# Linear attention and a Sinkhorn-routed expert layer: attention products in 64x64 quarters, another feature order of x^T, and a new written order of the front

## The chip, the cores and the metric

The kernel runs on one core of one Trainium2 chip. The metric is device time in microseconds of one execution; the median of several executions is compared. The profile is of one further execution. Engines are named as in the profile: PE is TensorE's matmul, PEld its weight load, DVE VectorE, ACT ScalarE, POOL GpSimd, SP SyncE. A matmul takes a stationary operand (up to 128 partitions by 128 columns, loaded by PEld) and a moving operand of up to 512 columns. PE can also be addressed in quarters of 64 rows by 64 columns.

## The reference

```python
def _attn_ref(q, k, v):                        # 8 batches, 8 heads, 576 tokens, 64 features
    q_p, k_p = phi(q), phi(k)                  # phi(x) = (x if x > 0 else exp(x) - 1) + 1
    kv  = np.einsum('bhsd,bhse->bhde', k_p, v)
    z   = np.sum(k_p, axis=2)
    num = np.einsum('bhsd,bhde->bhse', q_p, kv)
    den = np.einsum('bhsd,bhd->bhs', q_p, z)[..., None] + 1e-06
    return num / den
def _moe_ref(x, w_gate, w1, w2):               # 4608 tokens, 512 features, 8 experts, 1024 hidden
    P = np.exp(x @ w_gate - max)
    for _ in range(8):
        P /= P.sum(1, keepdims=True) + 1e-09
        P /= P.sum(0, keepdims=True) + 1e-09
        P *= N / E
    for e in range(E):
        out += P[:, e:e + 1] * (np.maximum(x @ w1[e], 0.0) @ w2[e])
    return out
```

The attention output, with the 8 heads side by side, is x.

## The kernel before

**Attention.** `att(b, g)` (L366) treats four heads of one batch; there are 16 such calls. Partition p of an input tile holds nine consecutive tokens; partitions 0 to 63 belong to one head and 64 to 127 to the next (index hh), and a second index r selects the heads 4 further on. ACT takes Exp of k and q (L398, L463), DVE forms max(x + 1, 1) and the minimum with the Exp (L402, L406, L466, L470), which is phi. `f_kv` (L422) sums k' times [v, ones] over nine token slices with matmuls of 64x64 stationary size, four per slice in the four quarters of PE; two banks of PSUM and both partition halves receive them. `f_z` copies the result to `kvz`, in two copies of 64 partitions each (L440 to L444, the second after the first), into the diagonal blocks of a tile whose other blocks GpSimd zeroes once (L619). `f_qt` (L451) transposes q' in quarters, and `f_qc` (L472) copies it to SBUF. `heads` (L484) then multiplies: for each hh one full-array matmul of 288 token columns, with the two heads r = 0, 1 on the diagonal blocks of the stationary operand. It is called four times an `att`: two halves of the tokens (c), once for the denominator (`den`, written to the tile `att`) and once for the numerator (`num`). ACT takes Ln of the denominator (L499) and Exp of its negative (L504); DVE multiplies the numerator with it into x^T (L514). The resulting x^T has the feature index (64 r + d) on partitions and 2 g + hh as its chunk, so w1 and w_gate are loaded in matching pieces of 64 partitions (`load_w1` L327, `f_wg` L599). Tokens stand in the order 64 j + w for the token 9 w + j.

**Experts.** The 4608 tokens are nine groups of 512. A unit is one expert on one group: layer 1 (x^T to hidden) and layer 2. Expert 0 runs in the front while attention is still going on: `layer1` (L679) is plain in groups 0 to 4 and `block7` (L877) uses seven products (Winograd's form) in place of eight in groups 5 to 8. `unit_plain` (L987) has the plain layer 2 of eight products, each of four 512-column matmuls (L998); `unit` (L1059) calls `layer2` (L1067) with seven products of eight 256-column matmuls (L1114), four DVE sums S of the hidden activations (L1085), a seed copy on ACT (L1166) and evictions, four of them copies and two adds (L1132). The constant NS = 4 makes units 4 to 7 of expert 0 use it. `combos` makes the weight sums W and T. After that, experts 1 to 7 run with seven products in both layers (`pair`, L806; `layer2`). `last` (L1191) is the last layer 2, plain, in tiles whose finishing DVE pass is L1219, and `out_dma` (L969) stores each tile in two halves of 64 token rows.

**What sets the order.** Nothing is scheduled at run time. `_Plan` (L17) collects tasks with an engine, an estimated duration, dependences and buffers, and issues them engine by engine. PE's `TURN` is what the plan assumes for a change between tasks with `cfg=0` and `cfg=1` (quarters). The first 1811 tasks follow `_FRONT` (L141), a list written out by hand: task number and engine letter (p PE, a ACT, d DVE, g POOL, s SP, m a landing, n none). What follows is chosen by the plan's estimates. So the list fixes the order on every engine, the loads on POOL's queue among them, up to expert 2. The waits themselves are semaphores, and the estimates have no part in them.

Quarters in PE's list today: 20 islands of kv and transposes among full-array work, 16 of them behind the first layer-1 matmul. On POOL's queue eight loads of q, k, v stand ahead of the first piece of the first w1, and two loads on SP's.

Of the kernel before, what the change touches and what calls it, by code (L numbers as in the profile page):

```python
# [11 lines left out]
FP16 = mybir.dt.float16  # L12
# [5 lines left out]
class _Plan:  # L18
# [4 lines left out]
    TURN = 0.13  # L23
# [118 lines left out]
50s 51m 108n 61n 1n 113n 2p 48s 49m 3p 4p 5p 6p 7p 8p 9p 10p 11p 12p 13p 14p 15p 16p 17p  # L142
18p 62a 63d 54a 0g 19p 20p 21p 22p 23p 24p 25p 26p 27p 64d 55d 28p 65p 78g 79m 89n 52g 53m 56d
90a 57n 58p 59d 60d 76g 77m 66a 29p 82a 30p 31p 120g 121m 131n 67p 68a 32p 33p 34p 35p 36p 37p 69p
38p 39p 40p 83d 91d 84d 132a 133d 92d 80g 81m 85n 86p 134d 87d 88d 70a 71a 118g 119m 41p 93p 94a 42p
43p 74p 125d 75d 124a 95p 72p 44p 122g 123m 146g 147m 45p 96a 73d 126d 127n 153d 46p 97p 98a 99a 128p 129d
130a 135p 136d 109g 110m 148g 149m 159n 100p 596p 137p 101d 150g 151m 152a 154d 138a 160a 47p 102p 103d 155n 161d 162d
597p 598p 139p 140a 141a 111g 112m 156p 157d 158a 174g 175m 163p 164d 176g 177m 187n 595n 599p 144p 145d 165p 166a 600p
602p 601d 604p 603d 606p 167p 142p 180a 605d 168a 178g 179m 114g 115m 608p 610p 609a 612p 181d 143d 182d 189d 188a 190d
202g 203m 204g 205m 215n 613d 183n 184p 185d 611a 191p 192d 169a 186a 607a 614p 632n 615a 172p 173d 206g 207m 193p 194a  # L150
208a 618p 170p 171d 209d 210d 217d 234g 235m 245n 211n 195p 616p 216a 218d 633p 635p 636d 634a 196a 212p 197a 213a 219p
220d 214d 637p 639p 246a 638a 116g 117m 232g 233m 236g 237m 247d 260g 261m 262g 263m 200p 221p 222a 248d 201d 239d 640d
619p 626a 617p 238a 240d 223p 641p 198p 224a 225a 624a 199d 292g 293m 104g 105m 241n 643p 644a 266a 267d 249p 642d 273n
242p 243d 244d 275d 250d 645p 646a 620p 622p 647p 290g 291m 318g 319m 106g 107m 264g 265m 251p 623p 303n 304a 294g 295m
274a 252a 305d 268d 226p 276d 227d 253p 621p 228p 269n 254a 255a 648d 229d 230p 270p 320g 321m 348g 349m 296a 231a 271a
297d 628d 325d 306d 666p 277p 278d 376g 377m 272a 258p 259d 668p 653p 279p 324a 331n 665n 298d 630d 346g 347m 332a 256p
257d 299n 667a 280a 654p 281p 322g 323m 282a 669d 333d 352a 283a 300p 307p 301d 670p 302d 671a 672p 308d 309p 310a 284p
326d 285d 334d 651p 311p 673a 312a 286p 359n 360a 287d 652p 353d 313a 335p 336d 374g 375m 327n 328p 329a 330a 288p 289a
661a 387n 389d 404g 405m 350g 351m 378g 379m 406g 407m 460g 461m 674p 469s 337p 338a 354d 361d 362d 462g 463m 470s 314p
315d 649p 339p 675a 388a 340a 659a 316p 355n 560d 381d 317d 650p 676p 356p 390d 357d 341a 363p 408g 409m 364d 655p 358a  # L160
342p 417n 411d 419d 343d 493g 494m 380a 678p 365p 656p 344p 677d 410a 464g 465m 432g 433m 491g 492m 471s 500s 501s 366a
561d 382d 383n 562d 345d 553d 367p 680p 698n 681d 663a 679a 368a 418a 699p 700d 391p 384p 392a 385a 420d 386d 701p 703p
369a 393p 394a 554d 702d 412d 495g 496m 502s 684p 372p 373d 439d 555d 434g 435m 438a 657a 395p 705p 396a 445n 370p 371d
685p 563s 564m 421p 440d 704d 413n 476n 414p 682p 692a 706a 397a 688p 415a 416d 422a 400p 447d 478d 401d 707p 498d 423p
446a 424a 708a 556s 557m 567d 568d 569d 436g 437m 503g 398p 399d 683p 709p 570s 571m 425p 689p 711p 448d 477a 497a 690d
426a 710a 427a 574d 575d 441n 442p 443a 479d 576d 449p 450d 686p 713p 444d 451p 499d 565s 566m 572s 573m 577s 578m 558s
559m 579s 580m 508n 509a 510d 712a 687p 428p 452a 714a 696a 581d 582d 429d 583d 740p 742p 584s 585m 588g 589n 739n 590g
591m 743d 453p 741a 454a 455a 430p 431d 511d 504n 744p 480p 481d 746p 456p 457d 402p 403a 505p 694a 466a 745d 467d 506d
507d 468d 735d 748p 747a 749a 512p 458p 459d 750p 752p 751d 513a 472n 514p 515a 473p 474a 736d 516p 475d 517a 518a 753a
754p 755d 721p 519p 737d 520d 482p 483a 722p 729a 521p 522d 738d 756d 757d 484p 485a 486a 719p 489p 490d 717p 720p 727a  # L170
718p 725a 487p 488d 551n 592n 593g 594m 1009s 1010m 1011s 1012m 1013s 1014m 1015s 1016m 758d 778d 586s 587m 1017s 1018m 731d 715p
716p 723a 785n 779d 762p 763a 760p 523p 552p 761a 524a 732d 836d 780d 786p 781s 782m 783s 784m 787a 525n 1019s 1020m 766p
790p 791a 800p 801a 733d 837d 734d 792p 788p 793a 802p 803a 806p 796p 526d 759d 1001d 789a 797d 838d 839s 840m 808p 804p
807a 767a 805a 794p 809d 795d 764p 798p 799a 810p 527p 1002d 811d 528d 770p 771d 844p 845a 846p 812p 847a 813a 768p 850p
851a 765a 772p 843n 854p 773a 529d 858p 848p 894d 1003d 1021s 1022m 1051s 1052m 1053s 1054m 860p 818p 852p 849a 855d 814d 769d
859a 864p 862p 819a 820p 865a 863a 861a 815d 1004d 824p 868p 825a 856p 816d 857a 821a 853d 866p 817d 895d 869d 530p 896d
828p 902p 903a 826p 870p 871a 867d 531d 908p 909a 829d 822p 830p 831a 906p 532d 823a 952d 533p 872d 827d 904p 912p 905a
901n 907a 876p 953d 878p 916p 917a 913d 914p 534d 873d 918p 922p 954d 877a 897s 898m 955s 956m 923a 910p 882p 535d 874d
899s 900m 841s 842m 926p 911d 915a 920p 919a 924p 879a 883a 921a 925d 875d 960p 536p 537d 927d 886p 887d 961a 966p 1055s
1056m 957s 958m 967a 880p 964p 884p 928p 929a 970p 962p 963a 888p 889a 974p 968p 959n 965a 538d 539p 885d 930d 936p 975a  # L180
971d 972p 973a 540d 969d 541d 980p 976p 977a 934p 881a 981a 935a 982p 1023p 978p 984p 542p 979a 931d 940p 1024a 983d 985d
543d 1025p 986p 1029p 941a 937a 1026a 932d 944p 1030a 1031p 1027p 1028a 1033p 987a 544d 938p 545p 1034d 1035p 1037p 1036a 1038a 1032d
945d 1039p 1040a 546d 547d 933d 946p 1043p 1044a 1045p 1041p 1047p 1065p 548p 549d 550d 1046d 947a 988p 942p 1000n 1057s 1058m 943d
1059s 1060m 1048d 1042a 1061s 1062m 1063s 1064m 1066a 989p 996a 1147s 1148m 1149s 1150m 1067p 1068a 990p 1049p 1071p 1050a 1072a 1151s 1152m
1513n 1514g 1515m 728d 1005d 1006d 629a 1121d 991p 997a 992p 892a 1073p 994p 1122d 1007d 1069p 1123d 1074d 1070a 625a 1075p 627d 697a
993p 1076d 1077p 691d 1079p 1081p 664a 1080a 631d 1008d 1082a 1078a 995p 1085p 1086a 1087p 1083p 1089p 1093p 1095p 1124d 999d 1090d 1088d
998d 1091p 1084a 1094a 1099p 1096a 939d 1101p 1097p 1125p 1127p 1128d 695d 1092a 1100a 1129d 1126a 1130p 1131a 1103p 1135p 1138p 1104d 1105p
1107p 1136d 1098a 775d 1139d 1137d 662a 1109p 1141p 1106a 1108a 1113p 1153s 1154m 1155s 1156m 1110a 1115p 1114a 1133a 730a 1132g 1134g 1157s
1158m 1111p 1102d 1117p 1161p 1163p 1112a 1142d 1140d 1116d 1143d 1144p 1118d 1119p 1159s 1160m 1269s 1270m 1271s 1272m 1273s 1274m 1516n 1517g
1518m 1162a 1167p 1164a 658a 1120a 1169p 1168a 1165p 1146d 1145d 1189d 1190d 1193p 1195p 1194a 1198p 1171p 1203p 1166a 660a 1191d 1192d 1197d  # L190
726d 1196d 1201a 1202g 1199a 1206p 1172d 1173p 1174a 1175p 1176a 1177p 1178a 1205d 1204d 1209p 1181p 1182a 1183p 1179p 724d 1185p 1207d 1170d
1211d 1208d 1210d 1186d 1215p 693a 1217p 1212p 1187p 1243d 1200g 1244d 1214d 777d 1213d 1245d 774d 1246d 1180a 1216a 1221p 832a 1218a 1223p
1219p 1247p 1249p 1222a 1250d 1224d 1251d 1220a 1248a 1252p 1255a 1256g 951a 1188a 1225p 1226d 1184d 1257p 1259d 1260p 1258d 1519d 893d 1261d
1227p 1228a 1229p 1230a 1231p 1232a 833a 1263p 1235p 1237p 1275s 1276m 1233p 1236a 1239p 1253a 1264d 1520d 1521d 1265d 1277s 1278m 1279s 1280m
1281s 1282m 1283p 1391s 1392m 1393s 1394m 1285p 1266p 1240d 1234a 1284a 1238d 1241p 1289p 1286a 1291p 1287p 1395s 1396m 1242a 835a 1268d 1262d
1267d 1315p 1290a 1316a 1311d 1317p 1320p 1312d 1313d 1321a 1319d 1318d 1314d 1293p 1325p 1328p 776d 1294d 1295p 1288a 1327d 1330d 1326d 1329d
# [25 lines left out]
def kernel(  # L222
# [139 lines left out]

    def att_bank():
        return at2[:, (len(p_att["order"]) - 1) % 2]

    def att(b, g):  # L366
        n = 2 * b + g
        pr = n - 100.0
# [961 lines left out]
```

## Time and profile before

| | us |
|---|---|
| median of 3 runs (lowest, highest) | 954.69 (954.31, 955.13) |
| the profiled execution | 955.01 |
| its span | 953.2 |
| start of the first layer-1 matmul on PE | 22.14 |
| start of the first block product of unit 5 | 124.02 |
| start of the first product of expert 1's third step | 191.27 |
| start of the last products of `last` | 947.16 |

Shares of the span: PE 99%, DVE 81%, ACT 61%, POOL 15%. The granted clock of PE is 1.0. By stages the shares differ: from 40 to 100 us DVE and ACT are busy about 94% of the time, after 200 us about 80% and 57%. How to read it: the three starts cut the span into a start-up, the attention stage, a stage in which expert 0's later units run beside the Sinkhorn iterations, and experts 1 to 7. Busy time of PE includes overlap of pipelined matmuls, so distances between starts are used for prices.

### The profile page before, as it was taken

The numbers are of one execution on the slowest core, as the hardware profiler recorded it, in microseconds if no ns is written. First come the engines' busy times: TensorE is split into PE (matmuls) and PEld (weight loads), VectorE is DVE, ScalarE is ACT, GpSimd is POOL, SyncE is SP. The second block draws the span as 40 slices with busy tenths as digits, with TensorE's granted clock in tenths as the row PEclk, the third lists the DMA queues.
The fourth block names the chain that finished last, engine by engine and source line by source line (L and its number), as shares of the span: only waits on it lengthen the run. The fifth ranks groups of instructions, "written<-read, shape, count | busy, mean of one in ns | idle before, by whom it ended". The sixth has DMA issues, their size and how long they took to land.

```text
span 953.2 us, 19767 instructions
## 1 busy us (share of the span) xinstructions
PE 939.4 (99%) x7728; PEld 645.9 (68%) x7728; DVE 775.3 (81%) x1500; ACT 582.3 (61%) x1033; POOL 144.6 (15%) x209
## 2 busy tenths in 40 slices
PE   7999999999999999999999999999999999999997
PEld 3555588666677666766677666766667666776665
DVE  7899899979887888778888888878887888877775
ACT  7999766766655555555555555555555555555552
POOL 6442000011111111111111111111112111111110
PEclk9999999999999999999999999999999999999999
DMA  9999863452244222652226222652226422215544
GB/s 245 256 252 198 192 164 106 122 122 79 78 115 91 78 78 78 161 122 79 78 78 128 79 78 79 150 108 64 76 67 147 112 78 79 73 45 166 166 133 133
DMA packets 81513, 112.73 MB, mean 118 GB/s; under 512 B 7436, under 2 KB 45196, under 8 KB 81420
## 3 DMA queue, kind: packets, MB, share of 16 engines
q1 hardware_dynamic: 56844, 75.65, 26.0%
q0 software_dynamic: 23856, 34.78, 19.5%
q8 instruction: 60, 0.98, 0.4%
q10 hardware_dynamic: 720, 1.05, 0.3%
q14 instruction: 33, 0.27, 0.1%
HBM read 119.69 MB, written 17.69 MB: 144 GB/s over the span
## 4 chain that ended last, share of the span: by engine, by line
PE 92%; ACT 3%; DVE 2%; DMA 1%; POOL 1%; issue 1%; DVEq 0%; ACTq 0%; POOLq 0%
PE ye L1114 36%; PE hq L818 24%; PE R L818 12%; PE Zye L1114 6%; PE Zye L818 6%; PE ye L998 2%; PE hq L703 2%; DMA w<-in_moe_w_dram 1%; ACT rden L499 1%; ACT eq L463 1%; PE num_ps L486 1%; PE att L486 0%; PE hq L1210 0%; DVE xT L514 0%; PE att L531 0%
## 5 line engine op out<-in xcount | busy, mean ns | idle before, releaser
L1145 DVE SCALAR_TENSOR_TENSOR acc<-ye,P_sb,acc 128x256 f32<-128x256 f32 x620 | 268.3, 480 | 126.9 <-PE ye L1114 125.0
L1114 PEld LDWEIGHTS <-S 128*128 128x128 f16 x1984 | 194.0, 98 | 46.6 <-DVE S L1085 0.2
L1114 PE MATMUL ye<-T,S 128*128 128x256 f16 x1488 | 192.8, 273 | 0.0
L1155 POOL TENSOR_TENSOR acc<-acc,st 128x256 f32<-128x256 f32 x124 | 88.2, 731 | 633.8 <-ACT st L1152 622.6
L1114 PEld LDWEIGHTS <-hb 128*128 128x128 f16 x1584 | 155.0, 98 | 43.0 <-issue 1.3
L818 PEld LDWEIGHTS <-W 128*128 128x128 f16 x1248 | 122.1, 98 | 86.0
L849 ACT ACTIVATE hb<-hq 128x512 f16<-128x512 f32 x134 | 80.0, 597 | 141.0 <-PE hq L818 135.7
L818 PE MATMUL R<-xs,W 128*128 128x512 f16 (+1 forms) x560 | 150.1, 358 | 0.0
L818 PE MATMUL hq<-xs,W 128*128 128x512 f16 (+1 forms) x560 | 150.1, 358 | 0.0
L818 PE MATMUL hq<-xs,w 128*128 128x512 f16 (+1 forms) x560 | 139.8, 358 | 0.0
L818 PEld LDWEIGHTS <-w 128*128 128x128 f16 x936 | 91.6, 98 | 59.3 <-issue 0.5
L846 ACT ACTIVATE hb<-Zye 128x512 f16<-128x512 f32 x134 | 80.1, 598 | 40.4 <-PE Zye L818 40.3
L1152 ACT ACTIVATE st<-Zye,P_sb 128x256 f32<-128x256 f32 x124 | 52.4, 470 | 76.7 <-PE Zye L1114 76.5
L852 DVE CUSTOM_DVE_ANT_0 hb<-hq,sx 128x512 f16<-128x512 f32 x126 | 86.6, 687 | 15.5 <-PE hq L818 15.3
L839 ACT COPY sx<-hq 128x512 f32<-128x512 f32 x126 | 73.5, 584 | 35.3 <-PE hq L818 35.3
L835 ACT COPY Zye<-hq 128x512 f32<-128x512 f32 x134 | 77.8, 580 | 21.1 <-PE hq L818 20.7
L852 DVE CUSTOM_DVE_ANT_0 hb<-R,sx 128x512 f16<-128x512 f32 x126 | 86.5, 686 | 4.8 <-ACT sx L839 3.8
L1085 DVE TENSOR_TENSOR S<-hb 128x1024 f16<-128x1024 f16 x124 | 85.0, 685 | 5.1 <-ACT hb L849 5.0
L818 PE MATMUL Zye<-xs,w 128*128 128x512 f16 (+1 forms) x280 | 75.0, 358 | 0.0
L843 ACT COPY sx<-R 128x512 f32<-128x512 f32 x126 | 74.4, 591 | 0.0
L1114 PE MATMUL ye<-w,hb 128*128 128x256 f16 x528 | 68.4, 273 | 0.6 <-DVE acc L1145 0.5
L1114 PE MATMUL Zye<-w,hb 128*128 128x256 f16 x528 | 68.4, 273 | 0.0
(120 smaller groups left out, 966.2 us busy)
## 6 DMA issues: line engine op xcount, KB each, us to landing
xs<-xd SPq DMA_DIRECT2D x196, 256.0 KB, 3.5
kin<-in_k_dram POOLq DMA_DIRECT2D x15, 576.0 KB, 7.3
w<-in_moe_w_dram POOLq DMA_DIRECT2D x16, 512.0 KB, 7.7
out_dram<-acc SPq DMA_DIRECT2D x63, 128.0 KB, 2.4
w<-in_moe_w_dram POOLq DMA_DIRECT2D x7, 1024.0 KB, 10.2
xs<-xd SPq DMA_DIRECT2D x49, 128.0 KB, 3.3
vv<-in_v_dram POOLq DMA_DIRECT2D x16, 288.0 KB, 7.2
hb<-in_q_dram POOLq DMA_DIRECT2D x15, 288.0 KB, 7.7
```

The lines of the kernel that those rows point to most:

```text
L818: nc.tensor.matmul(dst_[:, p, :] if parts == 2 else dst_.rearrange("p a b -> p (a b)"), lhsT=lhs(p, c), rhs=blk[i](c), start=(first and p ...
L835: nc.scalar.copy(out=Zt[1], in_=gX["tile"])
L839: nc.scalar.copy(out=gs2["tile"], in_=gX["tile"])
L843: nc.scalar.copy(out=gs5["tile"], in_=gR["tile"])
L846: nc.scalar.activation(out=dst(0, 0), in_=Zt[1], func=AF.Relu)
L849: nc.scalar.activation(out=dst(1, 0), in_=gX["tile"], func=AF.Relu)
L852: nc.vector._custom_dve(TENSOR_ADD_SAT, out=out_, in0=ps, in1=sb, s0=3.0e38, s1=0.0)
L1085: nc.vector.tensor_tensor(out=Sx[:, i], in0=a0, in1=a1, op=op)
L1114: nc.tensor.matmul(bank(g_)[:, s, :], lhsT=lhs(s, kk), rhs=rhs(kk), start=(new and s == 0 and kk == 0), stop=(kk == 3), skip_group_check=True)
L1145: nc.vector.scalar_tensor_tensor(out=dst(), in0=bank(g_)[:, s, :], scalar=P_sb[:, gg, e:e + 1], in1=dst(), op0=ALU.mult, op1=ALU.add)
L1152: nc.scalar.mul(out=gst["tile"], in_=bank(g_)[:, s, :], mul=P_sb[:, gg, e:e + 1])
L1155: nc.gpsimd.tensor_tensor(out=dst(), in0=dst(), in1=gst["tile"], op=ALU.add)
```

## The change

All in one file; the written list is replaced as a whole. In words:

- `heads` issues four 64x64 matmuls of 288 columns (hh by r) in place of two full-array ones, with `cfg=1`. Its output has hh on partition halves and r on banks. `kvz` has no zero blocks: one copy for `f_z`, and the two memsets on POOL go.
- x^T has features in their natural order (chunk g + 2 r, partition 64 hh + d). w_gate is one load of 128 partitions, the first expert's w1 two loads of 512 columns each (every feature), the later experts' w1 two loads of two chunks each. `layer1` sums chunks in the order 0, 2, 1, 3.
- In the last batch (b = 7) the copy `f_qc` brings tokens to their natural order, so group 8 is stored with one DMA a tile, on SP's and ACT's queues in turn.
- NS = 6: units 4 and 5 of expert 0 have the plain layer 2. The four W and four T sums are made ahead of unit 5.
- `last` ends with a 256-column and two 128-column tiles in place of two 256-column ones.
- The plan's estimates change, and `_FRONT` has 2192 entries. PE's list now has 51 islands of quarters (mostly two tasks, such as a num beside a den); 87 changes of mode lie behind the first layer-1 matmul, where there were 32. Seven loads stand ahead of the first w1 piece on POOL's queue. The copy `f_qc` of the last batch is on ACT, twice.

The core of the diff:

```diff
-    NS = 4
+    NR = B - 1
+    NS = 6
...
-    kvz_t = [fp.tile([P, 2, 2, P], FP16, ...
+    kvz_t = [fp.tile([P, 2, 2, D], FP16, ...
...
+            return load_w(moe_w1, "w1", p_w1, [[((slice(None), slice(None), slice(512 * i, 512 * i + 512)),
+                                                 512 * i, [[F, P], [P * F, NDT], [1, 512]])] for i in range(2)], e, ...
+        return load_w(moe_w1, "w1", p_w1, [[((slice(None), slice(2 * i, 2 * i + 2)), 2 * i * P * F, [[F, P], [P * F, 2], [1, F]])]
+                                           for i in range(2)], e, ...
...
-        for r in range(2):
-            def f_z(e, r=r):
-                s = slice(64 * r, 64 * r + 64)
-                src = gkv["tile"][s, :, 0:2 * D].rearrange("p h (z d) -> p h z d", z=2)
-                dst = gz["tile"][s, :, :, 64 * r:64 * r + 64]
-                copy(e, dst, src if r == 0 else src[:, :, ::-1])
+        def f_z(e):
+            copy(e, gz["tile"], gkv["tile"][:, :, 0:2 * D].rearrange("p h (z d) -> p h z d", z=2))
...
+            if b >= NR:
+                copy(e, gq["tile"].rearrange("p h (w j) -> p h w j", j=NJ), qps().rearrange("p h j w -> p h w j"))
...
         def heads(dst, c, z):
             for hh in range(2):
-                nc.tensor.matmul(dst[:, hh, 0:CH], lhsT=gz["tile"][:, hh, z, :],
-                                 rhs=gq["tile"][:, hh, :, :].rearrange("p j w -> p (j w)")[:, CH * c:CH * c + CH],
-                                 start=True, stop=True)
+                for r in range(2):
+                    nc.tensor.matmul(dst[half(hh), r, 0:CH], lhsT=gz["tile"][half(r), hh, r ^ z, :],
+                                     rhs=gq["tile"][half(r), hh, CH * c:CH * c + CH], start=True, stop=True)
...
-                nc.vector.tensor_tensor(out=xT[:, 2 * g:2 * g + 2, S * b + CH * c:S * b + CH * c + CH],
+                nc.vector.tensor_tensor(out=xT[:, g:NDT:2, S * b + CH * c:S * b + CH * c + CH],
...
-    for t in kvz_t:
-        nc.gpsimd.memset(t, 0.0)
...
-            t1 = add(("pe", 0.2175 * (c1 - c0)), f_hq, deps=[tw1[0 if c1 == 2 else 1], ...
+            t1 = add(("pe", 0.2175 * (c1 - c0)), f_hq, deps=[tw1[0 if g == 0 and f < 4 else 1], ...
...
-        for i, (tt, c0, cw) in enumerate(((3, 0, 512), (2, 0, 512), (1, 0, 512), (0, 0, 256), (0, 256, 256))):
+        for i, (tt, c0, cw) in enumerate(((3, 0, 512), (2, 0, 512), (1, 0, 512), (0, 0, 256), (0, 256, 128), (0, 384, 128))):
```

More of the change, by code (lines that the diff above doesn't have):

```diff
@@ L290 @@
     vv_t = [fp.tile([P, 3, NJ, D], FP16, tag=f"vv{i}", name=f"vv{i}", bufs=1) for i in range(NV)]
-    kvz_t = [fp.tile([P, 2, 2, P], FP16, tag=f"kvz{i}", name=f"kvz{i}", bufs=1) for i in range(2)]
+    kvz_t = [fp.tile([P, 2, 2, D], FP16, tag=f"kvz{i}", name=f"kvz{i}", bufs=1) for i in range(2)]
     kvps = front.enter_context(tc.tile_pool(name="kvps", bufs=1, space=PSUM))
@@ L364, in att_bank, with half @@
         return at2[:, (len(p_att["order"]) - 1) % 2]
+    def half(i):
+        return slice(64 * i, 64 * i + 64)
     def att(b, g):
@@ L472, in f_qc @@
         def f_qc(e):
[L473 to L474 removed]
+            gq["tile"] = fp.tile([P, 2, S], FP16, tag="qpT", name="qpT")
+            if b >= NR:
+                copy(e, gq["tile"].rearrange("p h (w j) -> p h w j", j=NJ), qps().rearrange("p h j w -> p h w j"))
+            else:
+                copy(e, gq["tile"], at2.bitcast(FP16)[:, :, 0:S])
         gtq = S_.grp(p_tq)
@@ L617 @@
         nc.vector.memset(t[:, 1], 1.0)
-    for t in kvz_t:
-        nc.gpsimd.memset(t, 0.0)
     att(0, 0)
     att(0, 1)
-    for r in range(2):
-        gsw = S_.grp(p_sw)
-        ti = add(("pool", 0.8), lambda _, r=r: f_wg(_, r), acq=[gsw], use=[gsw], prio=-96.5, after=1.75)
-        wg_done.append(add(("dma", 0.3), lambda _: None, deps=[ti], use=[gsw], prio=-96.5, lat=2.15))
+    gsw = S_.grp(p_sw)
+    ti = add(("pool", 0.8), f_wg, acq=[gsw], use=[gsw], prio=-96.5, after=1.75)
+    wg_done.append(add(("dma", 0.3), lambda _: None, deps=[ti], use=[gsw], prio=-96.5, lat=2.15))
     w_t = {0: load_w1(0, prio=-290.0, parts=2)}
@@ L701, in f_hq @@
                     ghq["tile"] = hqp.tile([P, 512], FP32, tag="hq", name="hq")
-                for c in range(c0, c1):
+                for i in range(c0, c1):
+                    c = (0, 2, 1, 3)[i]
                     nc.tensor.matmul(ghq["tile"], lhsT=gw1["tile"][:, c, ts(f, P)], rhs=xT[:, c, ds(512 * g, 512)],
-                                     start=(c == 0), stop=(c == NDT - 1))
+                                     start=(i == 0), stop=(i == NDT - 1))
             def f_rl(eng, f=f, ghq=ghq):
@@ L969, in out_dma, with f_o @@
     def out_dma(g, tt, deps, c0=0, cw=DM):
-        for half in range(2):
-            def f_o(_, half=half):
-                bb, j = divmod(2 * (4 * g + tt) + half, NJ)
-                dst = AP(tensor=out.tensor, offset=(S * bb + j) * DM + c0, ap=[[NJ * DM, PW], [1, cw]])
-                eng = nc.scalar if g >= NG - 2 and half == 1 else nc.sync
-                eng.dma_start(out=dst, in_=acc[g][64 * half:64 * half + 64, tt, c0:c0 + cw])
+        r0 = P * (4 * g + tt)
+        whole = r0 >= NR * S
+        n_out[0] += 1
+        for half in range(1 if whole else 2):
+            def f_o(_, half=half, eng=nc.scalar if (n_out[0] % 2 if whole else g == NG - 2 and half) else nc.sync):
+                bb, j = divmod(2 * (4 * g + tt) + half, NJ)
+                if bb >= NR:
+                    dst = AP(tensor=out.tensor, offset=(r0 + 64 * half) * DM + c0, ap=[[DM, P if whole else PW], [1, cw]])
+                else:
+                    dst = AP(tensor=out.tensor, offset=(S * bb + j) * DM + c0, ap=[[NJ * DM, PW], [1, cw]])
+                eng.dma_start(out=dst, in_=acc[g][64 * half:64 * half + (P if whole else 64), tt, c0:c0 + cw])
             add(("sp", 0.45), f_o, deps=deps, prio=900.0)
@@ L1002, in unit_plain @@
                              prio=g + 0.1 * (2 * tt + half) + 0.65)
-                if g == NG - 1:
-                    h_users[0].append(ty[tt])
-                    h_users[1].append(ty[tt])
+                if g >= NG - 2:
+                    for i in range(2):
+                        h_users[2 * (NG - 1 - g) + i].append(ty[tt])
         for tt in range(4):
@@ L1042, in combos @@
                      prio=-900.0 if e > 1 else 4.5)
-        for i in range(4):
+        for i in range(4 if e > 0 or NS < NG - 1 else 0):
             def f_T(_, i=i):
```

232 lines of the change are left out of this document (120 added, 112 removed).

## The prediction

> **What bounds the kernel now.** I read the page first, then busy time by stage, then TensorE's timeline, then the waits and the end. The stages are cut at three starts on TensorE: its first useful layer-1 matmul (22.14 us), the first block product of unit 5 (124.02) and the first product of expert 1's third step (191.27), from where both orders issue the same sequence.
>
> ```profile
> span 953.2 us, 19767 instructions
> ...
> PE 939.4 (99%) x7728; PEld 645.9 (68%) x7728; DVE 775.3 (81%) x1500; ACT 582.3 (61%) x1033; POOL 144.6 (15%) x209
> ```
>
> ```profile
> 22.14:124.02 101.88, 98.60 (x1502) 55.68 (x1503) 92.80 (x162) 88.44 (x123) 28.80 (x43) 1.00 1.02 225
> 124.02:191.27 67.25, 67.25 (x564) 54.62 (x563) 63.41 (x137) 45.36 (x85) 1.26 (x2) 1.00 0.45 121
> 191.27:947.16 755.89, 755.32 (x5383) 526.41 (x5382) 602.88 (x1173) 432.29 (x811) 100.03 (x140) 1.00 0.37 99
> ```
>
> Columns: stage, length, then busy us of PE, PEld, DVE, ACT, POOL, granted clock, DMA share, GB/s. TensorE (PE) is the bound everywhere. Behind 191.27 nothing that it does changes until the last tiles, so that stage keeps its length. What can change is the start (22.14), the attention stage, where VectorE (DVE, 91%) and ScalarE (ACT, 87%) are close behind PE, the second stage, and the end. The profiled execution took 955.01 us, 1.8 more than its span; the median of the runs shown is 954.69. I sum against 955.0.
>
> **Prices on PE.** Starts are the safe figure, since ends are modelled.
>
> ```profile
> 72.24 1.03 PE L998 MATMUL ye<-w,hb 128*128 128x512 f16 x4
> 73.11 1.03 PE L703 MATMUL hq<-xT,w 128*128 128x512 f16 x4
> 74.06 0.70 PE L428 MATMUL kv_ps<-vv,t 64*64 64x128 f16 x36
> 74.59 0.48 PE L456 MATMUL att<-ident,tq 64*64 64x64 f16 x36
> 75.00 1.04 PE L998 MATMUL ye<-w,hb 128*128 128x512 f16 x4
> 75.88 0.41 PE L486 MATMUL num_ps<-qpT,kvz 128*128 128x288 f16 x2
> 76.12 1.03 PE L703 MATMUL hq<-xT,w 128*128 128x512 f16 x4
> ```
>
> Four 512-column matmuls take 0.866 (73.11-72.24). The same four ahead of the quartered kv take 0.95: entering quarters costs 0.09. kv alone is 0.53 (74.06 to 74.59). The quartered transposes take 0.41 when full-array work follows, and 0.35 where kv follows (80.81 to 81.16 in the same timeline): leaving costs 0.06; after kv it costs 0.10 (81.16 to 81.79, less 0.53). I take **0.09 a turn**, bounds 0.06 and 0.13. A call of `heads` is 0.245 (75.88 to 76.12).
>
> **Head calls.** A call becomes four 64x64 matmuls of 288 columns. No row shows that; kv is nearest, also quartered, also into two partition halves and two banks: 36 matmuls of 128 columns in 0.53 are 14.7 ns each, so four of 288 columns are 4 x 14.7 x 288/128 = **0.13 us**. By the transposes (0.35/36 = 9.7 ns for 64 columns) it would be 0.175; the other end is today's 0.245, or 0.48 if the four run singly (four halves of today's call of two). By kv, the 57 of 64 calls behind the first layer-1 matmul save 57 x 0.115 = 6.6.
>
> **Turns.** Walking the written order: today 20 islands of quartered work in the front, 16 of them behind the first layer-1 matmul, 32 turns. The new order has 51 islands, mostly pairs such as num beside den, and 87 turns behind that point. 55 more turns x 0.09 = +5.0. Most of what the quarters save is paid back here.
>
> The Trainium skill (TensorEngine Tiling (Array Packing), Key Properties) says that a change of tiling mode drains TensorE, which speaks against every island; it gives no figure, and by a drain as long as a head matmul's whole way (0.286 in its row, less the 0.12 between starts: 0.165) the 55 turns would cost an estimated 9.1 in place of 5.0. The starts above show 0.06 to 0.10, so the trace has a drain but a shorter one.
>
> **Units 4 and 5 plain.** A Winograd layer 2 is 7 products of 0.873, a plain one 8 of 0.866: 2 x (6.93 - 6.11) = +1.6. What goes from the other engines is larger: eight S sums on DVE (0.68 each), four adds on DVE (0.68) and two seeds on ACT (0.58): 9.3 us; the copies to SBUF stay eight. One filler matmul fewer: -0.2. Today's list from the first layer-1 matmul to 191.27, each task at its distance between starts, is: 40 layer-1 groups of four 512-column matmuls and 40 such plain layer-2 halves (0.866), 28 Winograd products (0.873), 83 block products (0.436 or 0.433), 57 head calls, 13 kv, 13 transposes (at 0.31, the shortest), 4 logits (0.88), 8 Sinkhorn sums (0.145) and two small ones: 160.0. With 32 turns that is 162.9 of the 169.1 that the stage lasts, so **6.2 us are waits**. After: -6.6 + 1.6 - 0.2 + 5.0 = **-0.2**.
>
> **Waits.** These are small gaps on evacuations, both ways:
>
> ```profile
> DVE xT L514 <- PE num_ps L486: 5.3, 11, 0.8
> ...
> ACT rden L499 <- PE att L486: 5.5, 12, 0.7
> ...
> ```
>
> (DVE's and ACT's waits, 0 to 130 us: in total, times, longest.) The kvz copies were two in series (DVE 0.42, ACT 0.36) between kv and the first head call; now one of the same width on all partitions. That (13 copies of about 0.39 in these stages, 5.1) and the plain units (9.3) lighten DVE and ACT by about 14 us between them; about half of it falls to DVE's second stage, which is 94% full today. With PE's work unchanged and the two others lighter, PE waits less: eight gaps of 0.2 or more have a named releaser, 2.8 together, and 1.2 of that is kvz or qpT copies. Bounds 1.6 (the named gaps left) and 6.2; I take half, 3.1: **-3.1**.
>
> **Start.** Layer 1 waits for the first expert's weights:
>
> ```profile
> 9.60 12.40 DMA w<-in_moe_w_dram
> ...
> 22.14 0.59 PE L703 MATMUL hq<-xT,w 128*128 128x512 f16 x2 [0.22 <-DMA w<-in_moe_w_dram]
> ```
>
> The first line is from the chain, the second from the timeline. Ten loads of q, k or v and the first w1 piece (1 MB of source, 1.78 loads) land by 22.0; the first load, issued at 0.74, lands 3.9 later, so its transfer starts near 3.0: 19.0/11.8 = 1.6 us a load. The DMA share is over 1 then. The new order puts nine ahead: -1.6. GpSimd also loses two memsets (0.98 of POOL ahead of its first load), of which I count half: **-2.1** in all, bounds 0 and -4. The piece is now a column half, so products 0 to 3 need no second piece. Products 4 to 7 need one; if it is late that is up to 1.6 x 1.78 = 2.8, inside the range.
>
> **End.**
>
> ```profile
> 947.33 0.89 PE hq L1210 x8
> 948.21 0.03 issue
> 948.24 0.48 DVE acc L1219
> ```
>
> The last DVE pass has half the columns: from 0.75 (512) and 0.48 (256), 0.345, so -0.14. Two stores follow now, issued at 948.9 and 949.2, the second behind ScalarE's earlier issue (0.55 each); then there is one, on alternating queues: -0.3. I take **-0.5**, bounds 0 and -0.8.
>
> **At nothing.** The contraction order and views of xT: same matmuls. The last batch's strided qpT copy goes to ACT, twice; ACT has 15.0 of 20 us busy from 100 to 120, so 5 us cover it, and without them 0.5 to 1 each. Later experts' w1 in two full-width loads: median 10.2 us to land for 1 MB against some 108 us an expert (755.9/7).
>
> **Sum.** 955.0 - 2.1 (start) - 0.2 (PE's work) - 3.1 (waits) - 0.5 (end) = **949.1**.
>
> **Rivals.** *Cheap turns:* at 0.06 a turn (the transposes' row) 55 turns save 1.7 more, and waits of 1.6 another 1.5: 945.9. For it: DVE and ACT get lighter just where they are fullest. Against: islands of one or two calls have less to hide a drain than 36 matmuls.
>
> *Evacuation paces the front:* DVE and ACT are 91% and 87% busy there and each output of a head call still has to pass Ln or the multiply, so the waits stay at 6.2: 952.2; if the weights come no sooner either, 954.3. For it: those two stages leave DVE and ACT little room. Against: the two waits shown, where they wait for PE's head calls, and 14 us less work on them. The Trainium skill (TensorEngine Tiling (Array Packing), PSUM Bottleneck) names this: tiling speeds TensorE, not the evacuation.
>
> *Quarters do not run side by side (slower):* the change would not do what it says. The four have different moving data and two share each column half, in another sequence than kv's; if column halves take turns (0.245) and each waits for its own weight load (0.10, the 98 ns of LDWEIGHTS), a call is 0.345: 57 x 0.215 = +12.3, 961.4. It decides from 0.13 + 5.9/57 = 0.23 a call. Against: kv's 14.7 ns for 128 columns, of which one alone takes 53 (0.216/512 a column), can't be had without nearly four at once. The Trainium skill (TensorEngine Tiling (Array Packing), Restrictions) says that column tiling disables the fast weight load, so that four exposed loads of 107 ns a call would be an estimated 24 us; kv, with 36 loads and 36 matmuls in 0.53, shows such loads hidden.
>
> **How the numbers follow.** Forecast 0.53, cheap turns 0.17, evacuation 0.18, no overlap 0.10, none of these 0.02. About 0.2% (1.9 us) is what a measurement can tell from no change: below 952.8 is faster, above 956.6 slower. The forecast (nearly all), cheap turns and a third of evacuation are faster: 0.74; the rest of evacuation and a mild lack of overlap are the same: 0.15; slower 0.11. The range runs from just under cheap turns to the worse end of evacuation, 945.3 to 954.8.
>
> **What would show it.** Starts of an isolated head pair (num beside den) 0.26 apart plus 0.18 of turns, against 0.49 now; the first useful layer-1 matmul near 20.0; the first product of expert 1's third step near 186; PE's listed gaps from there back to the first layer-1 matmul about half; the last DVE pass 0.35 long. I would be wrong if a head call is over 0.2, if a turn is over 0.13 or if that layer-1 matmul does not come sooner.

## The result, and the profile after

After: 951.88 us, median of 6 runs (950.65 to 952.60). Before, on the same chip: 954.82 (954.18 to 957.16, 6 runs). The ratio is **0.9965**, 95% interval 0.9952 to 0.9978: faster by 2.9 us, about half of the 5.9 forecast. The profiled execution took 951.94 us against 955.01, with a span of 950.1 against 953.2.

The first lines of the page of after, and the same three stages as before, cut at the starts of the same three products (stage, length, busy us of PE, PEld, DVE, ACT, POOL, granted clock, DMA share, GB/s):

```profile
span 950.1 us, 19908 instructions
...
PE 939.9 (99%) x7816; PEld 631.7 (66%) x7816; DVE 765.3 (81%) x1479; ACT 575.8 (61%) x1025; POOL 144.3 (15%) x204
```

```profile
20.60:123.42 102.82, 99.82 (x1626) 47.03 (x1623) 86.32 (x149) 87.13 (x121) 30.09 (x41) 1.00 0.96 214
123.42:188.60 65.18, 65.18 (x513) 49.08 (x510) 60.60 (x132) 42.82 (x81) 1.41 (x2) 1.00 0.57 150
188.60:944.94 756.34, 755.77 (x5391) 526.86 (x5390) 603.24 (x1174) 432.60 (x811) 100.79 (x140) 1.00 0.37 99
```

Where the 3.1 us of the two spans went: the start is 1.54 shorter (22.14 to 20.60), the attention stage is 0.94 **longer** (101.88 to 102.82), the second stage is 2.07 shorter (67.25 to 65.18), and the third is the same: its mark, the start of the last products, belongs to a narrower tile now, but to the end of the last product it is 756.9 before (948.21 - 191.27) and 757.0 after (945.57 - 188.60). From there to the end of the span it takes 4.5 in place of 5.0.

The first two stages do not hold the same work before and after, so their lengths can't be compared as they stand. PE's matmuls of layer 2 in the attention stage, first before (three lines), then after (one):

```profile
L998 PE MATMUL ye<-w,hb 128*128 128x512 f16 x128 | 31.9, 379 | 0.0
L1114 PE MATMUL ye<-xT 128*128 128x256 f16 x8 | 1.0, 272 | 0.0
L1114 PE MATMUL ye<-w,hb 128*128 128x256 f16 x8 | 1.0, 272 | 0.0
```

```profile
L1017 PE MATMUL ye<-w,hb 128*128 128x512 f16 x152 | 37.1, 380 | 0.7 <-DMA w<-in_moe_w_dram 0.7
```

The new list has six groups of four 512-column matmuls more ahead of unit 5 (0.866 each, 5.2) and two seven-product ones fewer (0.873 each, 1.75): 3.45 us of PE's work moved from the second stage into the attention stage. For the same work, then, the attention stage is 2.5 shorter and the second stage 1.4 longer. The latter is what the two plain units cost (1.6) less the filler (0.2).

DVE's load in the attention stage fell from 92.8 to 86.3. DVE and ACT still wait for PE's calls there (0 to 130 us, total, times, longest; before, the totals were 5.3 and 5.5), so PE still sets the pace for most of it:

```profile
DVE xT L531 <- PE num_ps L504: 4.1, 7, 1.8
...
ACT rden L516 <- PE att L504: 5.3, 10, 1.2
```

What PE waits for, from the first layer-1 matmul to expert 1's third step (total, times, longest), first before (22.2 to 191.3), then after (20.7 to 188.6):

```profile
PE kv_ps L428 <- DMA vv<-in_v_dram: 0.5, 1, 0.5
PE hq L703 <- ACT hb L708: 0.5, 1, 0.5
PE att L531 <- DVE qpT L345: 0.5, 1, 0.5
PE att L486 <- ACT rden L499: 0.4, 2, 0.2
...
```

```profile
PE kv_ps L446 <- DMA vv<-in_v_dram: 1.0, 1, 1.0
PE ye L1017 <- DMA w<-in_moe_w_dram: 0.7, 1, 0.7
PE hq L717 <- DMA w<-in_moe_w_dram: 0.6, 1, 0.6
PE att L504 <- ACT kvz L359: 0.5, 1, 0.5
PE att L469 <- ACT P_sb L552: 0.3, 1, 0.3
```

The named waits (of before, four more of 0.2 to 0.4 follow) sum to the same, 3.0 and 3.1, but their kind has turned over: for what ACT and DVE make from 2.3 to 0.8, for landings of v and of the weights from 0.7 to 2.3. All of them lie in the attention stage; in the second stage the view lists none, before or after. The chain that ended last says it too: its shares by engine, first before, then after.

```profile
PE 92%; ACT 3%; DVE 2%; DMA 1%; POOL 1%; issue 1%; DVEq 0%; ACTq 0%; POOLq 0%
```

```profile
PE 94%; DMA 4%; ACT 1%; DVE 1%; POOL 0%; issue 0%
```

PE's timeline of after shows the new prices:

```profile
28.01 0.48 PE L469 MATMUL att<-ident,tq 64*64 64x64 f16 x36
28.43 1.04 PE L717 MATMUL hq<-xT,w 128*128 128x512 f16 x4
29.39 0.32 PE L504 MATMUL num_ps<-qpT,kvz 64*64 64x288 f16 x4
29.54 0.29 PE L504 MATMUL att<-qpT,kvz 64*64 64x288 f16 x4
29.76 1.04 PE L717 MATMUL hq<-xT,w 128*128 128x512 f16 x4
```

From 28.43 to 29.39 is 0.96 where four 512-column matmuls alone take 0.866: 0.09 to enter. The first call takes 0.15 until the second begins, the second 0.22 with leaving. A pair with its turns is 0.96 - 0.866 + 0.37 = **0.465 us**, against 0.49 for the two full-array calls of before. A single call with its turns is 0.335 at the least (0.085 to enter, 0.25 until the next full-array product begins), against 0.245. So a pair gains 0.025, and a single loses 0.09 or more.

The start and the end of after:

```profile
20.35 0.32 PE L504 MATMUL num_ps<-qpT,kvz 64*64 64x288 f16 x4 [0.16 <-DVE kvz L361]
20.60 1.04 PE L717 MATMUL hq<-xT,w 128*128 128x512 f16 x4
```

```profile
945.11 0.46 PE R L1229 x8
945.57 0.02 issue
945.59 0.35 DVE acc L1238
```

The first layer-1 matmul no longer has a wait for `w` in brackets; it follows the attention call ahead of it, which waited for DVE's copy of kvz.

### The profile page after: what moved, and what is told of

It is laid out like the page before. It is cut to its first block, busy times and chain, and to the rows that moved or that the text cites. A ratio compares the mean times of both kernels' runs of the same rounds, so it can differ in the third digit from the quotient of the medians.

```text
span 950.1 us, 19908 instructions
## 1 busy us (share of the span) xinstructions
PE 939.9 (99%) x7816; PEld 631.7 (66%) x7816; DVE 765.3 (81%) x1479; ACT 575.8 (61%) x1025; POOL 144.3 (15%) x204
## 4 chain that ended last, share of the span: by engine, by line
PE 94%; DMA 4%; ACT 1%; DVE 1%; POOL 0%; issue 0%
PE ye L1133 35%; PE hq L832 24%; PE R L832 12%; PE Zye L832 6%; PE Zye L1133 6%; PE ye L1017 5%; PE hq L717 3%; DMA w<-in_moe_w_dram 2%; DMA vv<-in_v_dram 2%; PE kv_ps L446 1%; PE att L504 0%; PE num_ps L504 0%; PE hq L1229 0%; DMA kin<-in_k_dram 0%; PE att L469 0%; PE R L1229 0%
## 5 line engine op out<-in xcount | busy, mean ns | idle before, releaser
L1133 PEld LDWEIGHTS <-hb 128*128 128x128 f16 x1536 | 150.3, 98 | 42.5 <-issue 1.3
L1133 PE MATMUL ye<-w,hb 128*128 128x256 f16 x512 | 66.3, 273 | 0.6 <-DVE acc L1164 0.5
L1133 PE MATMUL Zye<-w,hb 128*128 128x256 f16 x512 | 66.3, 273 | 0.0
```

Source lines behind the costliest of these rows:

```text
L1133: nc.tensor.matmul(bank(g_)[:, s, :], lhsT=lhs(s, kk), rhs=rhs(kk), start=(new and s == 0 and kk == 0), stop=(kk == 3), skip_group_check=True)
```

## The experiments

Each ratio is against the kernel before on the same chip; after itself stands at 0.9965. Theory: PE paces the front; what the quarters save in a call they give back in turns; DVE's and ACT's relief took their waits away, and landings took part of that room. No run has the new order without that relief, or the relief without the new order, so the part of each in the waits is argued and not shown. Rivals: the calls did not get cheaper; the turns cost nothing; ACT and DVE still pace the front; the start, the plain units or the end alone made the gain.

### Are the calls cheaper, and do they count?

`b_quart`: the kernel before, old order, with the quarter calls alone (the features of x^T and the weights' rows to match).

```diff
-                nc.tensor.matmul(dst[:, hh, 0:CH], lhsT=gz["tile"][:, hh, z, :], ...
+                for r in range(2):
+                    s, t = slice(64 * r, 64 * r + 64), slice(64 * hh, 64 * hh + 64)
+                    nc.tensor.matmul(dst[t, r, 0:CH], lhsT=gz["tile"][s, hh, r ^ z, :], ...
```

> The kernel before, in its old written order, with one part of the change alone: head calls of four 64x64 matmuls, x^T in feature order to suit, weights still in 64-partition pieces, two kvz copies as before. Theory (what quarters save is paid back in turns): the 57 calls behind the first layer-1 matmul fall from 0.245 to 0.146 us (-5.6); read with quartered head calls the old order has 101 turns there in place of 32, 69 more at 0.088 (+6.1); so within 1 us of the kernel before, 953.8 to 956. Rival (the quarters carry the gain of the change, the order is an extra): 3 us or more faster, 952 or less. Second rival (single short islands drain longer than pairs): 957 or more.

Measured: 956.88 us, 1.0022 (1.0012 to 1.0031). The quarters alone are worth nothing; in the old order they cost 0.2%. That is above the theory's range (to 956) and just short of the second rival's (from 957). In six of its eleven executions the mean granted clock is 0.995 to 0.997, against 0.998 or more in all of before's; the other five have a median of 956.36 (before's at 0.999 or more: 954.81).

```profile
22.83:125.93 103.10, 99.73 (x1615) 47.61 (x1616) 93.19 (x162) 88.76 (x123) 28.94 (x43) 1.00 1.01 222
125.93:193.18 67.25, 67.24 (x563) 54.63 (x562) 63.30 (x137) 45.36 (x85) 1.25 (x2) 1.00 0.44 120
```

The list, and so the work of each stage, is before's here. The start is 0.7 later, the attention stage 1.2 longer and the second stage the same. The gain of after needs the rest of the change.

`a_den2` and `b_den2`: every denominator call issued twice into the same bank, in after and in before (28 of them behind the first layer-1 matmul).

```diff
                 heads(at2, c, 1)
+                heads(at2, c, 1)
```

> The changed kernel with each denominator call issued twice, one right behind the other (the second overwrites the same values), so 32 calls and no turn are added; 28 of them lie behind the first layer-1 matmul. Theory (PE paces the front after 40 us): each costs its 0.146 us: +3.3 to +4.7 on 951.9, that is 955.2 to 956.6. Rival (evacuation by ScalarE and VectorE paces it, and PE's time is free there): under +1.5, below 953.4.

> The kernel before with each denominator call issued twice. Theory (PE paces the front of the kernel before as well, apart from 6 us of waits): 28 calls of 0.245 us behind the first layer-1 matmul are 6.9, of which the waits take in up to a third: +4.5 to +6.9 on 954.8, 959.3 to 961.7. Rival (evacuation paces it): under +2, below 956.8.

Measured: after with it 954.10, 0.9989 (0.9980 to 0.9998), which lies between the two forecasts (955.2 and more, 953.4 and less); before with it 960.14, 1.0053 (1.0039 to 1.0066), as the theory has it. The attention stage grew by 2.3 in after and by 5.3 in before. The second call of a pair of equal ones, first in after's trace, then in before's:

```profile
46.99 0.44 PE L504 MATMUL att<-qpT,kvz 64*64 64x288 f16 x8
47.26 0.29 PE L504 MATMUL num_ps<-qpT,kvz 64*64 64x288 f16 x4
```

```profile
80.84 0.65 PE L486 MATMUL att<-qpT,kvz 128*128 128x288 f16 x4
81.33 1.03 PE L999 MATMUL ye<-w,hb 128*128 128x512 f16 x4
```

Two calls take 0.27 in quarters (first 0.15, second 0.12) and 0.49 in the full array: a call costs half. PE's extra work, 28 x 0.12 = 3.4 and 28 x 0.245 = 6.9, comes through to two thirds and three quarters (2.3 and 5.3), so PE paces the stage for most of it; the rest fell into time in which it waited.

### What does a turn cost, and what does it buy?

`a_split`: after with nine pairs taken apart, and with them 120 turns for 102. Only the written list changes, as here for one pair (told by tasks; the list has their numbers):

```diff
-den(2)  num(1)  layer1  ...
+den(2)  layer1  num(1)  ...
```

> The kernel after with nine pairs of attention calls taken apart: the full-array task that followed the pair stands between its two calls. The same products, 120 turns in place of 102, and each single product still covered by full-array work. Theory that a turn has a price in PE's own time (a pair of calls with its turns took 0.47 us, a single call with its turns 0.335): nine times 0.20 is 1.8 us, so 0.998 to 0.9990 of the kernel before (after: 0.9965), with the stage before unit 5 longer by 1.3 to 2.2 us. Rival that the turns lie in time in which PE waits for landings and copies anyway: 0.9960 to 0.9975.

Measured: 953.87 us, 0.9985 (0.9976 to 0.9994), as the theory has it. The attention stage is 105.35, 2.53 longer, which is more than the 1.3 to 2.2 expected; but it began 0.62 sooner in this execution, and its end came 1.91 later, 0.21 a pair. The second stage is 65.17.

```profile
30.20 1.04 PE L717 MATMUL hq<-xT,w 128*128 128x512 f16 x4
31.17 0.32 PE L504 MATMUL num_ps<-qpT,kvz 64*64 64x288 f16 x4
31.52 1.02 PE L1017 MATMUL ye<-w,hb 128*128 128x512 f16 x4
32.48 0.32 PE L504 MATMUL att<-qpT,kvz 64*64 64x288 f16 x4
32.73 0.61 PE L1017 MATMUL ye<-w,hb 128*128 128x512 f16 x2
```

Its timeline shows what two singles cost: from 30.20 to 32.73 is 2.53, less two times 0.866 is 0.80, where a pair takes 0.465. The second of the two, 0.34 (31.52 to 32.73, less 0.866), is the usual one; the first is 0.11 dearer. Two of the usual ones cost 0.22 more than a pair.

`a_merge`: the other way, nine full-array tasks moved out from between two islands (84 turns for 102), with v of att(13) ahead of att(14)'s as in `a_v13` below.

```diff
-den(5.1) num(4.0)  layer1  qt(6) kv(6)  ...
+layer1  den(5.1) num(4.0) qt(6) kv(6)  ...
```

> The kernel after with v of att(13) loaded first, and in PE's list nine of the single full-array tasks that stand between two islands of quarters (from att5.den1 to att14.num1) moved to before the first of the two, so that the islands join: 84 turns in place of 102, the same products, and on the other engines nothing moved. Theory that a turn has a price of its own, some 0.09 us: 18 turns fewer are worth 1.6 us, nearly all of it before unit 5's first block product, so 0.993 to 0.9945 of the kernel before (the version with v first alone stood at 0.9954). Rival that the full-array tasks between islands are there as cover, and that without them PE waits for ACT's and DVE's copies instead: 0.9945 to 0.998, with waits of PE for kvz, qpT or att in the list that were not there.

Measured: 958.35 us, 1.0032 (1.0019 to 1.0045). The theory's 1.6 us of gain turned into a loss of some 7, worse than the rival's range too. PE's waits (20.3 to 195):

```profile
PE att L509 <- ACT rden L521: 4.1, 5, 0.8
PE att L474 <- ACT rden L521: 2.4, 3, 0.8
...
PE num_ps L509 <- DVE xT L536: 0.9, 1, 0.9
```

The attention stage is 109.52 against 102.17 in `a_v13`. Waits for Ln of the denominator, 6.5 in all, and for the multiply into x^T, 0.9, stand where there were none: two islands back to back ask for PSUM banks that ACT and DVE have not yet read. The full-array task between two islands is the time in which they do. So two turns have their price of some 0.2 us, and they buy cover worth more: joining these islands does not save it. Another way to join them was not tried.

### What is late after the change?

`a_v13`: after, with v of att(13) loaded ahead of that of att(14), their places on POOL's queue exchanged (and the marker that holds the later load back with them).

```diff
-448g 449m ... 421g 422m
+421g 422m ... 448g 449m
```

> The changed kernel with two loads of v changed about in the written order, so that the v of attention call 13 is loaded before that of call 14 and not last of all; the gate that holds back the stores of x blocks waits for the former in place of the latter. It takes away what TensorE waited for at 98.8 us (0.97 us for that v). Theory (landings are what is left of the waits, and TensorE is full behind them): 0.6 to 1.0 faster than the changed kernel, 950.9 to 951.3, and the gap gone from the trace. Rival (the next wait, on evacuation, takes its place): within 0.3 of 951.9.

Measured: 950.75 us (950.40 to 951.40), 0.9954 (0.9941 to 0.9966). The 1.0 wait for v is gone; the two front stages are 167.34 in place of 168.00, and the start was 0.4 sooner in this execution. It is the fastest kernel of the study and faster than before; the interval overlaps that of after, so against after it is the trace that speaks.

`a_lightv` and `b_lightv`: v of att(1) to att(4) loaded to a ninth (the rest keeps what the tile held, so the attention outputs of these calls differ), which frees DMA time in the first 40 us, in after and in before.

```diff
+                m = D if nm == "v" and 1 <= n <= 4 else NJ * D
...
-                    out=dst.rearrange("p r j d -> p r (j d)"),
+                    out=dst.rearrange("p r j d -> p r (j d)")[:, :, 0:m],
```

> The changed kernel with the v loads of attention calls 1 to 4 cut to a ninth of their bytes (the rest of those tiles holds ones, so the attention output of half of batch 0, of batch 1 and of half of batch 2 is not the reference's; everything else is computed as before). It takes about 3.6 loads, 5.7 us at 1.6 a load, out of the DMA queue of the first 40 us. Theory (in the new order the start and the waits up to 40 us are set by landings): the first layer-1 matmul and the two gaps on weights come sooner, 1.0 to 3 us faster, 949 to 951. Rival (the chain of attention work on ScalarE and VectorE sets the start, not the queue): within 0.5 of 951.9.

> The kernel before with the same four v loads cut to a ninth (the same parts of the output are not the reference's). Its first layer-1 matmul waited for weights by the trace, and its later gaps were on evacuations. Theory (landings set the start here too): the start comes 1 to 2 sooner, and some of it is lost again in evacuation gaps: 0.5 to 2 us faster, 952.8 to 954.3. Rival: within 0.5 of 954.8.

Measured: 951.07 us, 0.9956 (0.9943 to 0.9970), in after, between the two forecasts and not clear of after itself; 955.02, 1.0000 (0.9991 to 1.0009), in before, as the rival has it. In after the attention stage fell to 101.57, 1.25 less, and the waits for `w` went; part of it was lost to a start 1.1 later, where the theory had it sooner. The edit itself delays DVE: it first fills the whole v tiles, and its first pass over k begins at 6.62 in place of 4.65. Before, with the same edit, did not gain. So landings cost after some time in the front, and before none that shows; the size in after is not clean because of that start.

`a_w1`: `a_v13` with the second w1 piece directly behind the first on POOL's queue.

```diff
-w1 piece 0 | q att(3) | k att(3) | w1 piece 1
+w1 piece 0 | w1 piece 1 | q att(3) | k att(3)
```

> The kernel after with v of att(13) loaded first, and on POOL's queue the second piece of the first w1 directly behind the first, ahead of the loads of q and k of att(3). Theory that the landings of the weights are what PE still waits for after its start: the wait of 0.6 to 0.7 us for w in unit 0's layer 1 goes and the time stands at 0.9945 to 0.995 of the kernel before (v first alone: 0.9954). Rival that the loads of one queue only change places: att(3)'s q and k land 2 to 3 us later and PE waits 0.5 us or more for what is made of them, so 0.995 to 0.997.

Measured: 953.92 us, 0.9982 (0.9973 to 0.9991): against the theory, and worse than the rival. The waits for `w` are gone, and this is in their place, on ACT and then on PE:

```profile
24.71 1.16 ACT L482 ACTIVATE eq<-hb 128x1152 f16<-128x1152 f16 x1 [3.69 <-DMA hb<-in_q_dram]
25.78 0.72 ACT L521 ACTIVATE rden<-att,eps_t 128x576 f32<-128x576 f32 x1
```

```profile
26.56 0.32 PE L509 MATMUL att<-qpT,kvz 64*64 64x288 f16 x4 [1.54 <-ACT rden L521]
28.09 3.38 PE L722 MATMUL hq<-xT,w 128*128 128x512 f16 x8 [1.22 <-ACT hb L727]
```

ACT takes its list in order. It waits 3.69 for q of att(3); the Ln behind it, whose input had long been there, waits as well, and so does the relu of layer 1, and PE stands idle for 2.76. In `a_v13` the piece that lands late in front of PE is one wait of 0.7; here a load that lands late in front of ACT holds up all that is queued behind.

`a_ld8`: after with q of att(3) ahead of the first w1 piece, eight loads for seven.

```diff
-7 loads | w1 piece 0 | q att(3)
+7 loads | q att(3) | w1 piece 0
```

> The kernel after with one load more (q of att(3), 288 KB) ahead of the first w1 piece on POOL's queue, as it stood before: eight loads in place of seven. Theory that the start of layer 1 came sooner because the weights land sooner (the step of the prediction): the first layer-1 matmul starts between 21.5 and 22.2 in place of 20.6, and the time is 0.9972 to 0.9982 of the kernel before (after: 0.9965). Rival that in the new order attention's own chain sets that start and the weights have slack: the start stays within 0.3 of 20.6 and the time within 0.9960 to 0.9970.

Measured: 952.50 us, 0.9971 (0.9959 to 0.9982).

```profile
21.30 1.04 PE L717 MATMUL hq<-xT,w 128*128 128x512 f16 x4 [1.18 <-DMA w<-in_moe_w_dram]
```

The start is 0.7 later, with the weights as its releaser again. The time lies on the border of the two forecasts and the start a little under the theory's; but the row names the cause: one load more is enough to make the weights late again. In after, attention's chain and the weights come within less than a load's time of each other.

### Do the plain units and the narrow last tiles matter?

`a_ns5`: after with seven products in unit 5's layer 2 (its sums, seeds and evictions back in the list).

```diff
-    NS = 6
+    NS = 5
```

> The changed kernel with unit 5 back on seven products (NS = 5), its products put where the eight plain ones stood, its four sums, two adds and seed put beside them. TensorE has 0.82 us less to do, VectorE about 4.1 and ScalarE 0.6 more, in a stage where VectorE was busy 60.6 of 65.2. Theory (TensorE is full in that stage, so a plain layer 2 costs its eighth product): 0.4 to 0.8 faster than the changed kernel, 951.1 to 951.5. Rival (the plain units are what keeps VectorE from pacing that stage): slower by 0.5 to 3, 952.4 to 955.

Measured: 957.61 us, 1.0023 (1.0014 to 1.0032): against the theory, and worse than the rival's range (to 955). The profiled execution is the shortest of its runs, 955.62, at a mean clock of 1.0; eight of the eleven show 0.995 to 0.998.

```profile
144.67 0.39 PE L589 MATMUL R<-gs,ones_t 128*128 128x8 f32 x2 [0.74 <-DVE gs L584]
149.61 1.03 PE L1133 MATMUL ye<-xT,hb 128*128 128x256 f16 x8 [3.23 <-DVE acc L1151]
```

The second stage is 69.46 against 65.18. PE waits 3.23 for a bank that DVE has to empty, and 0.74 for the Sinkhorn sums in DVE's list. In this list the plain layer 2 costs PE 0.8 a unit and saves it four. But the kernel before has units 4 and 5 both on seven products, and its second stage lists no wait of PE. So seven products need not bring such waits. The list around the unit was written anew for this run, and how much of the waits is its order's is not known; another was not tried, and whether the plain units are worth their 1.6 us stays open.

`a_tail256`: after with two last tiles of 256 columns.

```diff
-(0, 256, 128), (0, 384, 128)
+(0, 256, 256)
```

> The changed kernel with the last tile in two 256-column pieces, as in the kernel before, and the new stores kept. Theory (the half-size last pass is worth its own length and little more): +0.1 to +0.3 on 951.9. Rival (the whole 0.45 us that the end gained comes from the tile size): +0.4 to +0.5.

Measured: 952.12 us, 0.9970 (0.9960 to 0.9980): 0.0005 from after, the rival's size, but not told from no change. In its trace the last pass is 0.48 again and the span ends 4.5 after the last product, as in after.

```profile
948.71 0.48 DVE acc L1238
```

So the 0.5 at the end does not come of the narrow tiles. What is left of the change there is the stores, one a tile on two queues in turn; that was not tried by itself.

## Why the prediction was right, and what was off

- **Head calls: right.** 0.12 to 0.15 a call against a forecast of 0.13. The rival that the quarters do not run side by side (0.345 a call) is out: the doubled calls cost 0.12. (By the price of 0.216 for 512 columns, a lone matmul of 128 takes 54 ns, not the 53 given; nothing hangs on it.)
- **Turns: right, a little low.** 0.09 was forecast and 0.09 is measured on entering, 0.10 on leaving (0.22 less a call of 0.12). Taken with the calls, an island of heads costs 0.025 more than forecast (0.465 against 0.44 for a pair, 0.335 against 0.31 for one); with 32 such islands behind the first layer-1 matmul that is 0.8. PE's work is then some +0.6 against the forecast -0.2. The cheap-turns rival is out.
- **Waits: the term that was mis-sized.** Forecast -3.1. The two stages last 168.00 in place of 169.13; with PE's work at 162.9 before and 163.5 after, the waits are 6.2 and 4.5: **-1.7**. This is a difference of sums and not a reading; the sign that was named, the listed gaps at about half, did not come (3.0 and 3.1). The direction is borne out by the named waits for ACT and DVE, which fell from 2.3 to 0.8. What I left out is what is late next: with PE no longer held by copies, it meets the landings of v, of the second w1 piece and of w2, 2.3 us of named waits where there were 0.7. I had costed the loads only at the start, with the second w1 piece as a possibility there. I also gave half of the relief to DVE's second stage, where PE had no wait to lose: with DVE busy 94% of it, the view lists none there before. So the plain units brought only their cost to that stage, and the saving in waits is all in the attention stage.
- **Start: right in kind, -1.5 for -2.1.** The weights did come sooner, and then attention's own chain was the next to be late, at 20.35; `a_ld8` shows the two close together.
- **End: right in size (-0.46 for -0.5), wrong in its parts:** the narrow tiles give nothing that shows.
- **Evacuation paces the front (952.2):** the nearest of the rivals in time, but not what happened: doubling a call lengthens the stage, and the waits left are mostly not ACT's and DVE's. The time alone would not tell: 951.9 is nearer to this rival than to the forecast of 949.1. And it is near: in `a_merge` and `a_ns5`, whose lists differ from the change's in places, PE waits for ACT or DVE at once.

With the measured terms: -1.5 + 0.6 - 1.7 - 0.5 = -3.1, the difference of the two spans (the waits were found as what is left, so the sum has to close). Against the forecast the start is short by 0.6, PE's work by 0.8 and the waits by 1.4.

How many of the 2.3 us of landing waits fall in any one execution stays open. In `a_tail256`, whose front is after's own, the wait for v was 2.0 and that for `w` 1.2, and its attention stage 106.35; that execution took 954.94, the longest of its kernel. Of the 3.5 us more than after's stage, 1.8 are named waits (4.9 for 3.1); behind the wait for v the clock was at half for 3.4 us, which is about the rest.

## What to carry to other kernels

Quarter-array products halve a small call, but each island pays about 0.09 on either side: a pair of calls just breaks even and a single one loses, so by these prices the saving comes only where several stand together. Do not then join islands without asking what the work between them covers: here it hid ACT's Ln, and moving it out cost 7.4 us where the turns it saved were worth 1.6. When an engine's load falls, list what is late next before counting the whole wait as gained, the loads' landings among it, and ask in which stage there is a wait to lose. And when the order changes, check that a stage holds the same work before comparing its lengths.

## What was not expected of the hardware

In `a_w1` PE stood idle from 25.0 to 28.1 but for one call, and its granted clock then fell (stretches of 1 us, columns as above):

```profile
27.00:28.00 1.00, 0.00 (x0) 0.00 (x0) 1.00 (x3) 1.00 (x3) 0.07 (x1) 0.86 1.22 204
28.00:29.00 1.00, 0.91 (x3) 0.35 (x3) 1.00 (x2) 1.00 (x3) 0.71 (x1) 0.50 1.25 209
...
31.00:32.00 1.00, 1.00 (x50) 0.60 (x52) 0.00 (x0) 0.65 (x1) 0.00 (x0) 0.93 1.25 217
```

The eight matmuls from 28.09 took 3.31 where eight take 1.73: 1.6 us more, on top of the 2.76 of waiting. Gaps of up to 1.0 in after left the clock at 1.00. The Trainium skill (TensorE: Matmul & The Clock Gate, What's actually happening) says that the clock is halved after an idle window of about 3.4 us and comes back after a busy one as long. The trace agrees on the half and on the 3.4 us back (27.7 to 31.1). On the idle window the runs differ, and they decide. In the 3.41 us ahead of the fall PE had been busy for 1.02 in `a_w1`, and for 0.91 in `a_tail256`, where the clock fell at 101.75 for 3.41 us. In the profiled execution of `a_ns5` it was busy for 0.19 of 3.41 us (146.2 to 149.6), and the clock stayed at 1.00. First `a_tail256` (a row of its timeline and one stretch of 1 us), then `a_ns5` (one stretch):

```profile
101.37 0.87 PE L446 MATMUL kv_ps<-vv,t 64*64 64x128 f16 x36 [2.03 <-DMA vv<-in_v_dram]
...
102.00:103.00 1.00, 1.00 (x14) 0.28 (x4) 0.71 (x3) 0.00 (x0) 0.00 (x0) 0.50 1.12 324
```

```profile
148.00:149.00 1.00, 0.00 (x0) 0.00 (x0) 1.00 (x4) 0.00 (x0) 0.00 (x0) 1.00 0.00 0
```

So a wait of 2.0 us can cost up to 1.7 more (half of 3.41), and a longer one need not. What decides it is open. 3.41 us at half are 0.0018 of an execution; ten of the eleven executions of `a_w1` show a mean clock of 0.997 or 0.998, where most of before's show 0.999 or 1.0.
